# Fixed PSUM turns beside the FFN, and other places in SBUF for buffers of its last batch

## The chip, the cores and the metric

One core of a Trainium2 chip runs the whole program. The metric is the device time of one execution in microseconds (us), the median of three runs. The core has five engines that run side by side and wait for each other only through semaphores: PE (TensorE, matmuls into PSUM), DVE (VectorE), ACT (ScalarE), POOL (GpSimd) and SP (SyncE, which here only issues loads). PSUM has eight banks of 512 fp32 values in each of 128 partitions, and this kernel uses all of them.

## The reference

Two parts follow each other. The first is a long convolution over the sequence (S = 12544, D = 128 channels, B = 4 batches), done by FFT, with a filter that a small MLP makes; the second is a maxout FFN on every token (50176 tokens, d_ff = 768).

```python
h_filt = (np.maximum(pos_emb @ w1, 0.0) @ w2) * np.exp(-0.01 * pos)[:, None]
u = x * v
y = irfft(rfft(u, n=2*S, axis=1) * rfft(h_filt, n=2*S, axis=0)[None], n=2*S, axis=1)[:, :S]
a = (x * y).reshape(B * S, D)
h = np.maximum(np.maximum(a @ w1, a @ w2), a @ w3)    # the FFN's own w1, w2, w3
out = h @ w_out
```

All data is fp32. The kernel folds the three-way maximum: with w1 taken off w2 and w3, `h = max(0, a(w2-w1), a(w3-w1)) + a w1`, and the last term goes through one 128x128 matrix `lin = w1 w_out`. So each step of the FFN is two matmuls, pa and pb, a relu of pa, and a maximum of that with pb.

## The kernel before

**Stages.** The first 321 us make the filter's spectrum and convolve batch 0. Then the FFN runs batch by batch. While the FFN of batch b runs, the convolution of batch b+1 is done beside it, in between its steps; the FFN of the last batch has nothing beside it and is computed in a Strassen-like form (seven products for eight), in pairs of tiles.

**Tiles and steps.** A batch has 32 tiles of 392 tokens. A tile starts with `t_load` (zt, the convolution's last but one stage from DRAM, and xT, the gate x), `t_sums` (a sum and a difference of zt's halves: `even` and zt), and `t_last`: 64 small matmuls with the table `f4p` into a PSUM tile `yps`, and DVE's product with xT into the SBUF tile `gt`, the FFN's input. Then come six steps f = 0..5 of `up` and `down`. `up` runs pa, the relu on ACT into `hid` (L701), pb, and the maximum on DVE (L704); `down`, two steps later, adds `hid` times a slice of `w_out` to the bank `ops`. After the last step ACT copies `ops` to the SBUF tile `ot` and POOL stores it. A matmul of `up` is done as two column halves that run at the same time (`halves_mm`, L154).

**The convolution beside it.** `conv_steps` lays out 192 slots, one per FFN step, and gives every piece of the next batch's convolution a slot, by hand-set loads. The pieces that use PSUM are `u_first` (tile ps1, the first transform), and `g_quarter` (tile psq: matmuls L462 of the forward and L472 of the inverse quarter transform), which `g_fold` reads with ACT (eo) and DVE (cb). `q_unfold` (L518, DVE) makes the input xs of L472.

**What sets the order.** The program text does: instructions are issued on each engine in the order in which Python makes them, and the framework adds the waits. A tile is taken from a pool with a tag and a number of buffers; which of the free buffers it gets is the framework's choice at the time of the build, by its own estimate of what is free, and a tile waits for all users of the buffer's tile before it. When a pool is closed, its memory is given to pools opened later, and their first writers wait for its last users.

**PSUM while the FFN runs.** Three banks belong to pool `hps` (tag `hps`: pa and pb), two double banks to `cps` (tag `cv`: ps1, psq and yps), one bank to `ops`. For the last batch the double banks are closed and three single banks (`cps2`, for yps) and two for the products are opened.

**SBUF.** After the first stage closes its pools (`pro.close()`, which frees `eye`, the weights `w_sb0`, the spectrum `specH` and more), the pool `hp` is opened and holds f4p, sign, zt, xT, even, gt and hid; f4p and sign are loaded on ACT's queue, in `hp`'s first bytes. The pools of the convolution follow, with `op` (ot) among them. When they close after the third batch, pool `lp` opens in their place with all that the last batch needs: the sums of weights `tw` and `linx` (five subtractions on DVE, L1090, ahead of the last batch's first step), its relu buffers (tags h11, h21, h22, h12), and its output buffers.

Of the kernel before, what the change touches and what calls it, by code (L numbers as in the profile page):

```python
# [1 line left out]

# [7 lines left out]
FP32 = mybir.dt.float32  # L10
I32 = mybir.dt.int32
U16 = mybir.dt.uint16
ALU = mybir.AluOpType
ACTF = mybir.ActivationFunctionType
PSUM = bass.MemoryType.PSUM
P = 128
# [8 lines left out]
N1 = 90  # L25
# [64 lines left out]
def kernel(  # L90
# [15 lines left out]
    nc = tc.nc  # L106
    NG, _, _, B, NB = x.shape
# [21 lines left out]
    f4p_d = nc.inline_tensor(np.ascontiguousarray(f4p_t), name="f4p_const").ap()  # L129
    wt_d = nc.inline_tensor(w_t, name="wt_const").ap()  # L130
    wq_d = nc.inline_tensor(wq_t, name="wq_const").ap()
    sign = np.where(np.arange(N1) < NK, 1, -1).astype(np.float32)[:, None]
    sign_d = nc.inline_tensor(sign.copy(), name="sign_const").ap()
# [6 lines left out]
    lin = const.tile([D, D], FP32, name="lin")  # L140
# [258 lines left out]
    def u_first(u, i0=0, n=4):  # L399


        t = uts[u] if i0 + n < 4 else uts.pop(u)
        ps = cps.tile([P, 256 * n], FP32, tag="cv", name="ps1")
        at = 4 * u + i0
        for i in range(n):
            for h in range(2):
                for c in range(2):
                    nc.tensor.matmul(  # L408
                        ps[64 * c:64 * c + 64, 256 * i + h * N1:256 * i + (h + 1) * N1],
                        t[:, 2 * ((at + i) % 8) + h].rearrange("n r t -> n (r t)"),  # L410
                        f1q[:, h, c * N1:(c + 1) * N1],
                        start=(i % 2 == 0 and h == 0), stop=True, skip_group_check=True)
        v = ps[:].rearrange("p (s m) -> p s m", m=256)[:, :, 0:2 * N1].rearrange(
            "p s (h k) -> p h k s", h=2)
        high = cvp.tile([P, n, D], FP32, tag="eo", name="high", bufs=2)
        high = high[:, :, 0:N1].rearrange("p s k -> p k s")
        nc.scalar.copy(high, v[:, 0])  # L417
        for a, op in enumerate((ALU.add, ALU.subtract)):
            nc.vector.tensor_tensor(out=spec[:, :, a, at:at + n], in0=v[:, 1], in1=high, op=op)  # L419
# [32 lines left out]
    def g_quarter(g, z):  # L452


        ps = cps.tile([P, 1024], FP32, tag="cv", name="psq")
        if g is not None:
            w, t = ws.pop((g, 0)), sqs.pop(g)
            for k in range(2):
                for r in range(2):
                    for a in range(2):  # L460
                        at = 512 * r + k * D
                        nc.tensor.matmul(  # L462
                            ps[64 * a:64 * a + 64, at:at + D], w[64 * r:64 * r + 64, k, a, :],
                            t[64 * r:64 * r + 64, k, a, :], start=(k == 0), stop=True,
                            skip_group_check=True)
        if z is not None:
            w, ab = ws.pop((z, 1)), abs_.pop(z)
            for q in range(2):
                for a in range(2):
                    for k in range(2):  # L470
                        at = 512 * a + 256 + q * D
                        nc.tensor.matmul(  # L472
                            ps[64 * k:64 * k + 64, at:at + D], w[64 * a:64 * a + 64, k, q, :],
                            ab[64 * a:64 * a + 64, q, k, :], start=(g is None and q == 0),
                            stop=True, skip_group_check=True)
        pss[g, z] = ps
# [160 lines left out]
    N = 4 * NB  # L637
# [38 lines left out]

    def t_last(i):
        zt = zts.pop(i)
        ps = cps.tile([P, state["yps"]], FP32, tag="cv", name="yps")
        own = i[0] == B - 1 and i[1] > 1  # L680
        g = (lp if own else hp).tile([D, 4, NB], FP32, tag="g", name="gt", bufs=4 if own else 3)
        y = ps[:, 0:N].rearrange("d (p n) -> d p n", p=4)

        h = NB // 2
        for s in range(4):
            for a in range(2):
                halves_mm(y[:, s, a * h:a * h + h], zt[a][:, s * D:(s + 1) * D],
                          f4p[:, i[0] > 0 and i[1] >= NT // 2, a, :], s == 0 and a == 0, True)
        y = y.rearrange("d p (a m) -> d p m a", a=2)
        xT = xTs.pop(i)  # L690
        nc.vector.tensor_tensor(out=g[:].rearrange("d p (m a) -> d p m a", a=2), in0=y,  # L691
                                in1=xT.rearrange("d p (m a) -> d p m a", a=2),
                                op=ALU.mult)
        gs[i] = g

    def up(i, f, tag="hid", bufs=3):
        rhs = gs[i][:].rearrange("d p n -> d (p n)")
        h = (lp if tag[0] == "h" and tag != "hid" else hp).tile([P, N], FP32, tag=tag, name="hid", bufs=bufs)
        pa = hps.tile([P, 512], FP32, tag="hps", name="pa")
        halves_mm(pa[:, 0:N], w_sb[1][:, f * P:(f + 1) * P], rhs, True, True)  # L700
        nc.scalar.activation(h[:], pa[:, 0:N], Relu)  # L701
        pb = hps.tile([P, 512], FP32, tag="hps", name="pb")
        halves_mm(pb[:, 0:N], w_sb[2][:, f * P:(f + 1) * P], rhs, True, True)
        nc.vector.tensor_tensor(out=h[:], in0=h[:], in1=pb[:, 0:N], op=ALU.max)  # L704
        return h
# [20 lines left out]
    NC = NF // 2  # L726
    ORDER = (("h11", 0), ("h21", 0), ("h11", 1), ("h22", 0), ("h21", 1), ("h11", 2),
             ("h21", 2), ("h22", 1), ("h22", 2), ("h12", 0), ("h12", 1), ("h12", 2))
    BUFS = {"h11": 3, "h21": 4, "h22": 4, "h12": 3}
# [167 lines left out]
    for i in (1, 2):  # L897
        nc.vector.tensor_tensor(out=w_sb[i][:], in0=w_sb[i][:], in1=w_sb[0][:],
                                op=ALU.subtract)
# [3 lines left out]
    cvp = pro.enter_context(tc.tile_pool(name="cvp0", bufs=3))  # L903
    cps = pro.enter_context(tc.tile_pool(name="cps0", bufs=3, space=PSUM))
    gps = pro.enter_context(tc.tile_pool(name="gps", bufs=2, space=PSUM))
    sps = pro.enter_context(tc.tile_pool(name="sps", bufs=1, space=PSUM))
    state = {"cv": (cvp, cps), "turn": cps, "xb": 2}
    pl = sps.tile([D, 512], FP32, name="pl")
    Gs, minus = {}, {}

# [103 lines left out]
    pro.close()  # L1014


    hp = ctx.enter_context(tc.tile_pool(name="hp", bufs=3))
    conv = ExitStack()
    f4p = hp.tile([N1, 2, 2, NB // 2], FP32, name="f4p", bufs=1)
    nc.scalar.dma_start(f4p[:], f4p_d)  # L1020
    sign_t = hp.tile([N1, 1], FP32, name="sign", bufs=1)
    nc.scalar.dma_start(sign_t[:], sign_d)
    inq = conv.enter_context(tc.tile_pool(name="inq", bufs=1))
    op_ = conv.enter_context(tc.tile_pool(name="op", bufs=2))
    wp = conv.enter_context(tc.tile_pool(name="wp", bufs=3))
    hh = conv.enter_context(tc.tile_pool(name="hh", bufs=2))
    cvp = conv.enter_context(tc.tile_pool(name="cvp", bufs=3))
    hps = ctx.enter_context(tc.tile_pool(name="hps", bufs=3, space=PSUM))
    cps = conv.enter_context(tc.tile_pool(name="cps", bufs=2, space=PSUM))
    ops = conv.enter_context(tc.tile_pool(name="ops", bufs=1, space=PSUM))  # L1030
    state = {"yps": 1024}


    tiles = [(b, i) for b in range(B) for i in range(NT)]
# [40 lines left out]


    lp = ctx.enter_context(tc.tile_pool(name="lp", bufs=1))
    cps = ctx.enter_context(tc.tile_pool(name="cps2", bufs=3, space=PSUM))
    state["yps"] = 512
    ops = ctx.enter_context(tc.tile_pool(name="ops2", bufs=1, space=PSUM))  # L1080
    banks = [ops.tile([P, 512], FP32, name=f"ops{i}") for i in range(2)]

# [2 lines left out]
    linx = lp.tile([D, 64], FP32, name="linx", bufs=1)  # L1085
    b11, b12 = wo_sb[:, 0:NC, 0:64], wo_sb[:, 0:NC, 64:128]
    b21, b22 = wo_sb[:, NC:, 0:64], wo_sb[:, NC:, 64:128]
    for out, a, b in ((tw[:, 1], b22, b12), (b12, b12, b11), (tw[:, 0], b22, b12),
                      (tw[:, 2], b21, tw[:, 0]), (linx[:], lin[:, 0:64], lin[:, 64:128])):
        nc.vector.tensor_tensor(out=out, in0=a, in1=b, op=ALU.subtract)  # L1090

    stream = {}

# [4 lines left out]
    for i in range(0, NT, 2):  # L1098
        h = {}
        X, Y = banks if i % 4 == 0 else banks[::-1]  # L1100
        for j, (name, f) in enumerate(ORDER):
            n = int(name[1]) - 1
            if j < 2 and i + 2 < NT:
                t_load(b, i + 2 + j)
            h[name, f] = first if step == 0 else up(
                (b, i + n), f + (NC if name[2] == "2" else 0), name, BUFS[name])
            if j == 0:
                entries = products(b, i, h, X, Y)
                for q, e_ in enumerate(entries):
                    at_ = step + LAG + q * NSTEP // len(entries)  # L1110
                    for fn in e_:
                        if isinstance(fn, tuple):
                            later(at_ + 1, *fn)
                        elif fn is not None:
                            later(at_, fn)
                for at_, (fn, c) in SUMS.items():
                    later(step + at_, fn, h, c)
            run(stream.pop(step, ()))
            if j in (3, 6) and i + 2 < NT:
                t_sums((b, i + 2 + (j > 3)), nc.vector)  # L1120
            if j in (5, 8) and i + 2 < NT:
                t_last((b, i + 2 + (j > 5)))
            step += 1
# [39 lines left out]
```

## Time and profile before

Times: 2338.91 us, the median of 2336.47, 2338.91 and 2343.64. The profiled execution took 2339.31 us, with a span of 2337.5 us and a mean granted PE clock of 0.996.

| stretch of the span, us | length | PE busy | DVE busy | ACT busy | POOL busy | DMA share |
|---|---|---|---|---|---|---|
| 340 to 820 (FFN beside the convolution) | 480.00 | 471.06 | 336.04 | 268.09 | 211.09 | 0.90 |
| 820 to 830 (end of batch 0) | 10.00 | 6.95 | 5.25 | 1.52 | 3.16 | 0.11 |
| 830 to 1911.65 (FFN beside the convolution) | 1081.65 | 1073.13 | 775.97 | 582.27 | 376.16 | 0.90 |
| 1911.65 to 1925 (start of the last batch) | 13.35 | 9.86 | 6.18 | 2.87 | 3.75 | 0.13 |
| 1925 to 2330 (last batch) | 405.00 | 404.78 | 193.54 | 102.96 | 263.29 | 0.22 |

The table sums each engine's busy time in a stretch. A busy PE in it is one whose matmuls follow each other; their ends are modelled, so two that overlap count once, and a gap between starts tells more than the busy share. Lines of the timeline begin with start and duration in us, then the engine, the line of the kernel, the operation, what is written and read, the shape, and how many are merged; in square brackets stands how long the engine was idle before it and what ended that. "SPq" and "ACTq" are the queues that issue loads. Names lose their numbers, so ps1 is shown as ps.

### The profile page before, as it was taken

The numbers are of one execution on the slowest core, as the hardware profiler recorded it, in microseconds if no ns is written. First come the engines' busy times: TensorE is split into PE (matmuls) and PEld (weight loads), VectorE is DVE, ScalarE is ACT, GpSimd is POOL, SyncE is SP. The second block draws the span as 40 slices with busy tenths as digits, with TensorE's granted clock in tenths as the row PEclk, the third lists the DMA queues.
The fourth block names the chain that finished last, engine by engine and source line by source line (L and its number), as shares of the span: only waits on it lengthen the run. The fifth ranks groups of instructions, "written<-read, shape, count | busy, mean of one in ns | idle before, by whom it ended". The sixth has DMA issues, their size and how long they took to land.

```text
span 2337.5 us, 68165 instructions
## 1 busy us (share of the span) xinstructions
PE 2284.1 (98%) x27853; PEld 1371.9 (59%) x27853; DVE 1553.8 (66%) x2798; ACT 1178.8 (50%) x2124; POOL 969.0 (41%) x1153
## 2 busy tenths in 40 slices
PE   8999989999999999999999999999999999999998
PEld 7889856655455445655555546655555546666665
DVE  5678856656777746757888846757888855454443
ACT  2678844456666624446666634446666622222222
POOL 1045424424444424324333324324333326666666
PEclk9999999999999999999999999999999999999999
DMA  7868969989998749979999849969999822222221
GB/s 160 201 202 266 290 158 181 165 180 238 226 238 219 198 104 187 188 141 238 240 248 246 226 113 180 192 144 244 242 241 245 223 80 66 54 54 70 65 55 22
DMA packets 473146, 410.93 MB, mean 176 GB/s; under 512 B 328004, under 2 KB 374231, under 8 KB 472834
## 3 DMA queue, kind: packets, MB, share of 16 engines
q1 hardware_dynamic: 433504, 317.61, 62.2%
q0 software_dynamic: 26400, 75.72, 11.2%
q10 hardware_dynamic: 12930, 13.25, 1.8%
q8 instruction: 219, 3.59, 0.7%
q14 instruction: 93, 0.76, 0.1%
HBM read 262.77 MB, written 84.67 MB: 149 GB/s over the span
## 4 chain that ended last, share of the span: by engine, by line
PE 76%; DMA 11%; DVE 5%; issue 3%; ACT 2%; SPq 1%; POOL 0%; ACTq 0%; DVEq 0%; POOLq 0%
PE pa L154 18%; PE pb L154 17%; PE ops L154 14%; PE ops L764 6%; PE ps L408 5%; DMA ht<-hd 4%; PE yps L154 4%; PE ps L163 3%; PE ps L154 2%; DMA zt<-zd 2%; PE psq L472 2%; DVE xs L518 2%; PE psq L462 2%; DMA sq<-spec 2%; DMA wt<-wq_const 1%
## 5 line engine op out<-in xcount | busy, mean ns | idle before, releaser
L701 ACT ACTIVATE hid<-pa 128x392 f32<-128x392 f32 x768 | 383.5, 499 | 756.5 <-PE pa L154 738.3
L704 DVE TENSOR_TENSOR hid<-hid,pb 128x392 f32<-128x392 f32 x768 | 428.2, 558 | 361.9 <-PE pb L154 351.5
L154 PE MATMUL pb<-gt,w_sb 128*64 128x392 f32 x3072 | 640.3, 495 | 10.2 <-ACT hid L701 10.2
L154 PE MATMUL pa<-gt,w_sb 128*64 128x392 f32 x3072 | 644.8, 497 | 0.7 <-DVE gt L691 0.7
L154 PE MATMUL ops<-hid,wo_sb 128*64 128x392 f32 x2304 | 478.1, 493 | 0.0
L154 PEld LDWEIGHTS pb<-gt,w_sb 128*64 128x64 f32 x3072 | 220.6, 137 | 301.2 <-issue 263.2
L514 POOL TENSOR_TENSOR cb<-cb,xs 128x512 f32<-128x512 f32 x135 | 176.3, 1306 | 455.1 <-DVE xs L511 210.5
L154 PEld LDWEIGHTS ops<-hid,wo_sb 128*64 128x64 f32 x2304 | 167.0, 137 | 212.9 <-issue 212.9
L154 PEld LDWEIGHTS pa<-gt,w_sb 128*64 128x64 f32 x3072 | 200.6, 137 | 147.6 <-issue 124.4
L419 DVE TENSOR_TENSOR spec<-ps,high 128x360 f32<-128x360 f32 (+1 forms) x204 | 142.1, 739 | 131.2 <-ACT high L417 130.8
L487 DVE TENSOR_TENSOR cb<-psq,eo 128x512 f32<-128x512 f32 (+1 forms) x288 | 175.3, 650 | 75.1 <-ACT eo L484 74.6
L719 POOL DMA_DIRECT2D out_dram<-ot x96 | 75.3, 785 | 322.2 <-ACT ot L717 293.7
L502 ACT ACTIVATE xs<-cb 32x512 f32<-32x512 f32 x270 | 169.9, 629 | 22.2 <-DVE cb L487 13.4
L518 DVE TENSOR_TENSOR xs<-cb 128x256 f32<-128x256 f32 x270 | 167.5, 662 | 9.8 <-POOL cb L514 9.8
L503 ACT COPY xs<-cb 32x512 f32<-32x512 f32 x270 | 166.7, 617 | 3.2
L417 ACT COPY high<-ps 128x360 f32<-128x360 f32 (+1 forms) x102 | 77.2, 761 | 157.2 <-PE ps L408 126.3
L408 PEld LDWEIGHTS ps<-f1q,uT 98*64 98x64 f32 x3072 | 131.8, 137 | 35.2 <-issue 32.9
L154 PEld LDWEIGHTS yps<-f4p,even 90*64 90x64 f32 x2048 | 116.1, 139 | 40.9 <-issue 35.0
L408 PE MATMUL ps<-f1q,uT 98*64 98x90 f32 x3072 | 136.4, 241 | 3.2 <-DVE spec L419 2.6
L691 DVE TENSOR_TENSOR gt<-yps,xT 128x392 f32<-128x392 f32 x128 | 72.3, 565 | 91.7 <-PE yps L154 52.6
L154 PE MATMUL yps<-f4p,even 90*64 90x49 f32 x2048 | 125.7, 221 | 3.0 <-DMA f4p<-f4p_const 3.0
L154 PE MATMUL yps<-f4p,zt 90*64 90x49 f32 x2048 | 127.3, 223 | 0.0
(130 smaller groups left out, 3306.7 us busy)
## 6 DMA issues: line engine op xcount, KB each, us to landing
ht<-hd SPq DMA_DIRECT2D x264, 256.0 KB, 6.7
wt<-wq_const SPq DMA_DIRECT2D x144, 256.0 KB, 6.4
zd<-cb POOLq DMA_DIRECT2D x135, 256.0 KB, 6.2
zt<-zd SPq DMA_DIRECT2D x384, 90.0 KB, 3.1
sq<-spec SPq DMA_DIRECT2D x264, 128.0 KB, 7.0
ut<-in_xr_dram SPq DMA_DIRECT2D x128, 196.0 KB, 4.3
ut<-in_vr_dram SPq DMA_DIRECT2D x128, 196.0 KB, 4.6
xT<-in_x_dram SPq DMA_DIRECT2D x256, 98.0 KB, 3.6
```

The lines of the kernel that those rows point to most:

```text
L154: nc.tensor.matmul(out[64 * h:64 * h + 64], lhsT[:, 64 * h:64 * h + 64], rhs, start=start, stop=stop, skip_group_check=True)
L408: nc.tensor.matmul(ps[64 * c:64 * c + 64, 256 * i + h * N1:256 * i + (h + 1) * N1], t[:, 2 * ((at + i) % 8) + h].rearrange("n r t -> n (r ...
L417: nc.scalar.copy(high, v[:, 0])
L419: nc.vector.tensor_tensor(out=spec[:, :, a, at:at + n], in0=v[:, 1], in1=high, op=op)
L487: nc.vector.tensor_tensor(out=cb[:, a, lo:hi], in0=ps[:, lo:hi], in1=eo[:, lo:hi], op=op)
L502: nc.scalar.mul(xs[at:at + 32], xt[at + 32:at + 64], -1.0)
L503: nc.scalar.copy(xs[at + 32:at + 64], xt[at:at + 32])
L514: nc.gpsimd.tensor_tensor(out=xts[g], in0=xts[g], in1=xs[:], op=ALU.add)
L518: nc.vector.tensor_tensor(out=ab[:, q], in0=y[:, 0], in1=y[:, 1], op=(ALU.subtract, ALU.add)[q])
L701: nc.scalar.activation(h[:], pa[:, 0:N], Relu)
L704: nc.vector.tensor_tensor(out=h[:], in0=h[:], in1=pb[:, 0:N], op=ALU.max)
L764: nc.tensor.matmul(ps[64 * c:64 * c + 64, 0:H2], w, rhs[:, H2 * c:H2 * c + H2], start=start, stop=True, skip_group_check=True)
```

## The change

Four things change; what is computed, and the instructions that compute it, stay the same.

1. The PSUM tiles of the FFN and of what runs beside it become fixed tiles that are used in strict turns: `hbanks` cycles over three single banks for pa, pb, pa, pb and so on; `pairs` cycles over two double banks for ps1, psq and yps; `singles` over three single banks for yps in the last batch. A matmul into such a tile waits for the readers of that tile alone. The first stage keeps its pool behind the same call (`state["bank"]`).
2. `hid` moves to a pool of its own, `hidp`, opened ahead of `hp`. f4p and sign thereby lie 4704 bytes higher, where specH was, and are loaded on SP's queue ahead of the first zt instead of on ACT's.
3. The pool `op` of ot is opened outside the convolution's pools, so its memory is not given to `lp`. The first three relu buffers of the last batch (steps 0 to 2) come from `hidp` instead of `lp`.
4. The five subtractions that make `tw` and `linx` are no longer made ahead of the last batch's first steps but one each behind `up` in steps 3 to 7.

The purpose is that no tile waits for a buffer that only the choice of the pool gave it, and that the last batch can start while the last store of the batch before is still under way.

```diff
         t = uts[u] if i0 + n < 4 else uts.pop(u)
-        ps = cps.tile([P, 256 * n], FP32, tag="cv", name="ps1")
+        ps = state["bank"]()[:, 0:256 * n]
         at = 4 * u + i0
...
                         start=(i % 2 == 0 and h == 0), stop=True, skip_group_check=True)
-        v = ps[:].rearrange("p (s m) -> p s m", m=256)[:, :, 0:2 * N1].rearrange(
+        v = ps.rearrange("p (s m) -> p s m", m=256)[:, :, 0:2 * N1].rearrange(
             "p s (h k) -> p h k s", h=2)
...
     def g_quarter(g, z):
-        ps = cps.tile([P, 1024], FP32, tag="cv", name="psq")
+        ps = state["bank"]()
         if g is not None:
...
         zt = zts.pop(i)
-        ps = cps.tile([P, state["yps"]], FP32, tag="cv", name="yps")
+        ps = state["bank"]()
         own = i[0] == B - 1 and i[1] > 1
...
         rhs = gs[i][:].rearrange("d p n -> d (p n)")
-        h = (lp if tag[0] == "h" and tag != "hid" else hp).tile([P, N], FP32, tag=tag, name="hid", bufs=bufs)
-        pa = hps.tile([P, 512], FP32, tag="hps", name="pa")
+        h = (hidp if tag == "hid" else lp).tile([P, N], FP32, tag=tag, name="hid", bufs=bufs)
+        pa = next(hbanks)
         halves_mm(pa[:, 0:N], w_sb[1][:, f * P:(f + 1) * P], rhs, True, True)
         nc.scalar.activation(h[:], pa[:, 0:N], Relu)
-        pb = hps.tile([P, 512], FP32, tag="hps", name="pb")
+        pb = next(hbanks)
         halves_mm(pb[:, 0:N], w_sb[2][:, f * P:(f + 1) * P], rhs, True, True)
...
     sps = pro.enter_context(tc.tile_pool(name="sps", bufs=1, space=PSUM))
-    state = {"cv": (cvp, cps), "turn": cps, "xb": 2}
+    state = {"cv": (cvp, cps), "turn": cps, "xb": 2,
+             "bank": lambda: cps.tile([P, 512], FP32, tag="cv", name="ps1")}
     pl = sps.tile([D, 512], FP32, name="pl")
...
     pro.close()
+    hidp = ctx.enter_context(tc.tile_pool(name="hidp", bufs=3))
     hp = ctx.enter_context(tc.tile_pool(name="hp", bufs=3))
+    f4p = hp.tile([N1, 2, 2, NB // 2], FP32, name="f4p", bufs=1)
+    nc.sync.dma_start(f4p[:], f4p_d)
+    sign_t = hp.tile([N1, 1], FP32, name="sign", bufs=1)
+    nc.sync.dma_start(sign_t[:], sign_d)
+    op_ = ctx.enter_context(tc.tile_pool(name="op", bufs=2))
     conv = ExitStack()
-    f4p = hp.tile([N1, 2, 2, NB // 2], FP32, name="f4p", bufs=1)
-    nc.scalar.dma_start(f4p[:], f4p_d)
-    sign_t = hp.tile([N1, 1], FP32, name="sign", bufs=1)
-    nc.scalar.dma_start(sign_t[:], sign_d)
     inq = conv.enter_context(tc.tile_pool(name="inq", bufs=1))
-    op_ = conv.enter_context(tc.tile_pool(name="op", bufs=2))
     wp = conv.enter_context(tc.tile_pool(name="wp", bufs=3))
     cvp = conv.enter_context(tc.tile_pool(name="cvp", bufs=3))
-    hps = ctx.enter_context(tc.tile_pool(name="hps", bufs=3, space=PSUM))
-    cps = conv.enter_context(tc.tile_pool(name="cps", bufs=2, space=PSUM))
+    hps = ctx.enter_context(tc.tile_pool(name="hps", bufs=1, space=PSUM))
+    cps = conv.enter_context(tc.tile_pool(name="cps", bufs=1, space=PSUM))
     ops = conv.enter_context(tc.tile_pool(name="ops", bufs=1, space=PSUM))
-    state = {"yps": 1024}
+    hbanks = itertools.cycle([hps.tile([P, 512], FP32, name=f"hps{i}") for i in range(3)])
+    pairs = itertools.cycle([cps.tile([P, 1024], FP32, name=f"cps{i}") for i in range(2)])
+    state = {"bank": lambda: next(pairs)}
     tiles = [(b, i) for b in range(B) for i in range(NT)]
...
     lp = ctx.enter_context(tc.tile_pool(name="lp", bufs=1))
-    cps = ctx.enter_context(tc.tile_pool(name="cps2", bufs=3, space=PSUM))
-    state["yps"] = 512
+    cps = ctx.enter_context(tc.tile_pool(name="cps2", bufs=1, space=PSUM))
+    singles = itertools.cycle([cps.tile([P, 512], FP32, name=f"last{i}") for i in range(3)])
+    state = {"bank": lambda: next(singles)}
     ops = ctx.enter_context(tc.tile_pool(name="ops2", bufs=1, space=PSUM))
...
     b21, b22 = wo_sb[:, NC:, 0:64], wo_sb[:, NC:, 64:128]
-    for out, a, b in ((tw[:, 1], b22, b12), (b12, b12, b11), (tw[:, 0], b22, b12),
-                      (tw[:, 2], b21, tw[:, 0]), (linx[:], lin[:, 0:64], lin[:, 64:128])):
-        nc.vector.tensor_tensor(out=out, in0=a, in1=b, op=ALU.subtract)
+    weights = [(tw[:, 1], b22, b12), (b12, b12, b11), (tw[:, 0], b22, b12),
+               (tw[:, 2], b21, tw[:, 0]), (linx[:], lin[:, 0:64], lin[:, 64:128])]
     stream = {}
...
                 t_load(b, i + 2 + j)
+            own = (name, BUFS[name]) if step > 2 else ("hid", 3)
             h[name, f] = first if step == 0 else up(
-                (b, i + n), f + (NC if name[2] == "2" else 0), name, BUFS[name])
+                (b, i + n), f + (NC if name[2] == "2" else 0), *own)
+            if step > 2 and weights:
+                out, a1, a2 = weights.pop(0)
+                nc.vector.tensor_tensor(out=out, in0=a1, in1=a2, op=ALU.subtract)
             if j == 0:
```

More of the change, by code (lines that the diff above doesn't have):

```diff
@@ L1 @@
+import itertools
 from contextlib import ExitStack
```

## The prediction

> **What bounds the kernel now.** I read the page first: PE is busy 2284.1 of 2337.5 us (98%), DVE 66%, ACT 50%. In the two FFN parts matmul blocks start every 0.66 us, each block being two column halves of 392 columns that run side by side, and between 1925 and 2330 us PE is busy 404.78 of 405.00 us. So time can only come from the few gaps on PE. The view of waits on PE names them (us in total, times, longest):
> ```profile
> PE pb L154 <- ACT hid L701: 10.2, 12, 3.5
> PE psq L472 <- DVE xs L518: 9.6, 15, 1.0
> ...
> PE yps L154 <- DMA f4p<-f4p_const: 3.0, 1, 3.0
> PE psq L472 <- DVE gt L691: 3.0, 1, 3.0
> ```
> Row 1 is a matmul that waits for a relu to empty its PSUM bank (one entry is 3.5, the rest about 0.6 each), row 2 a quarter transform that waits for its data. The timeline then shows each kind. First a short one:
> ```profile
> 614.56 0.83 PE L154 MATMUL pb<-gt,w_sb 128*64 128x392 f32 x4
> 615.87 0.83 PE L154 MATMUL pa<-gt,w_sb 128*64 128x392 f32 x4
> 617.30 0.88 PE L154 MATMUL pb<-gt,w_sb 128*64 128x392 f32 x4 [0.60 <-ACT hid L701]
> ```
> The second pb starts 1.43 us after its own pa instead of 0.66: both were put in the same bank, so it waits until the relu (L701) has read pa. Next the change to the last batch, all engines:
> ```profile
> 1912.70 0.76 POOL L719 DMA_DIRECT2D out_dram<-ot  x1 [11.30 <-ACT ot L717]
> 1912.96 0.83 PE L154 MATMUL pa<-gt,w_sb 128*64 128x392 f32 x4
> 1916.60 0.36 DVE L1090 TENSOR_TENSOR tw<-wo_sb 128x192 f32<-128x192 f32 x1 [5.42 <-DMA out_dram<-ot]
> 1916.70 0.89 ACT L701 ACTIVATE hid<-pa 128x392 f32<-128x392 f32 x2 [4.31 <-DMA out_dram<-ot]
> 1917.25 1.57 PE L154 MATMUL pb<-gt,w_sb 128*64 128x392 f32 x4 [3.46 <-ACT hid L701]
> ...
> 1918.62 1.52 PE L154 MATMUL pa<-gt,w_sb 128*64 128x392 f32 x4
> ...
> 1923.56 0.27 PE L154 MATMUL yps<-f4p,even 90*64 90x49 f32 x4
> ```
> The weight sums and the relu write SBUF that the closed convolution pools gave back, that of the output buffer ot among it; they wait until its last store has landed, and PE waits for the relu. After the gap the blocks start 1.37 and 1.30 us apart. The start of the first FFN:
> ```profile
> 320.51 1.92 SPq L645 DMA_DIRECT2D zt<-zd  x2
> ...
> 324.22 0.63 ACTq L1020 DMA_DIRECT2D f4p<-f4p_const  x1
> ...
> 325.53 0.69 DVE L669 TENSOR_TENSOR even<-zt 90x512 f32<-90x512 f32 x1 [0.30 <-DMA zt<-zd]
> 326.26 0.69 DVE L670 TENSOR_TENSOR zt<-zt 90x512 f32<-90x512 f32 x1
> 327.11 0.46 PE L154 MATMUL yps<-f4p,even 90*64 90x49 f32 x4 [3.05 <-DMA f4p<-f4p_const]
> ```
> The table f4p lands last, but `even` was ready only 0.9 us earlier (326.22).
>
> **What the skill says.** "PSUM — Partial Sum Buffer", PSUM bank collisions: access by two engines must be guarded by bank and quadrant, not by address. That is why a pb in its pa's bank has to wait for the whole relu; the trace agrees (pb starts 0.05 us after the relu's end). The same page, Engine vs sequencer instructions: the VectorE and ScalarE queues are strict FIFO; the trace agrees: the max at 1918.19 stands behind five weight sums. "TensorE: Matmul & The Clock Gate", Part 1: after an idle window of about 3.4 us the array runs at half clock until it has been busy about as long; the trace agrees (1.30 against 0.66 us). "Perfetto Trace Analysis", Identifying the Most-Contended Engine: repeated equal bubbles can mean too few buffers. Here the number is enough, the choice of buffer makes the bubble.
>
> **The change, part by part.** The order of instructions is the same on PE, ACT and POOL but for the two table loads, which go from ACT's queue to SP's; on DVE the five sums move. What changes is waits and addresses. I compared both built programs' waits, instruction by instruction, and placed each new wait on the times of this trace.
>
> 1. *Three FFN banks in turns.* The order is pa, pb, pa, pb, so pb of step k takes the bank of pa of step k-1 (waits for that relu) and pa of step k the bank of pb of step k-2 (waits for that max). In the kernel before, 10 of the 768 pairs share one bank: pa at 343.7, 346.5, 615.9, 746.6, 870.5, 873.3, 1395.9, 1398.7 (pb 1.43 later) and 571.9, 702.6 (1.73 later). Against 0.66 that is 8 x 0.77 + 2 x 1.07 = 8.3 us. The blocks after them start 0.71 instead of 0.66 later: 10 x 0.05 = 0.5. In turns pb needs the relu before, which in these ten places ended 0.8 us or more ahead of it. **Gain 8.8.**
> The turns also bind. At 1118, 1199, 1295, 1643, 1725 and 1821 us the max that pa must now await ends 0.67 us after pa's start. One of them:
> ```profile
> 1198.84 0.83 PE L154 MATMUL pa<-gt,w_sb 128*64 128x392 f32 x4
> 1198.97 0.55 DVE L704 TENSOR_TENSOR hid<-hid,pb 128x392 f32<-128x392 f32 x1
> 1199.58 0.88 PE L154 MATMUL pb<-gt,w_sb 128*64 128x392 f32 x4
> ...
> 1203.00 0.45 PE L472 MATMUL psq<-xs,wt 64*64 64x128 f32 x8 [0.41 <-DVE xs L518]
> ```
> That is 6 x 0.67 = 4.0 lost. But DVE runs without a pause there from 1196.3, and 3 us later psq waits for DVE anyway (starting 0.65 late at four of the six, 0.45 at two: 3.5 in all); a later PE meets the same DVE. Net 0.5, less the 0.06 waits of pb that go: **0.3 lost**, bounds 0 and 4.0. All other new waits on PE have 0.7 us or more to spare (but for pa at 1918.62, whose max comes earlier with part 3), those on ACT 1.3 or more, so they cost nothing.
> 2. *Two double banks in turns* (psq, yps, ps1): with two buffers in alternation the same reader is awaited; no wait of PE on another engine is new. **0**; the 3.0 us at 820 stays, since psq there needs the bank of yps either way.
> 3. *First relu buffers, ot and the sums of the last batch.* Relu 578 and 579 now wait for maxima that ended 2.6 us or more before them, and the sums stand one per step behind the max, waiting for nothing. From pa at 1912.96 to yps at 1923.56 it took 10.60 us; eight blocks at 0.66 take 5.3. Gain 5.3, of which DVE may take back up to 0.6: a step is 1.31 us and carries 0.56 + 0.36 on DVE, plus the two sums of zt (0.68 and 0.69 to 1.39) before yps. **Gain 5.1.** The sums are needed from step 9 on and are done in step 7.
> 4. *f4p and sign on SP's queue, ahead of zt.* f4p waits for the same fold matmul that zt waited for (320.4), so it starts at 320.51 and takes 0.63, sign 0.34. Every load behind them (zt, xT) moves 0.97. f4p then lands at 320.51 + 2.8 = 323.3, off the path, but zt lands at 326.5, `even` ends at 327.2, the difference at 327.9 and yps ends at 329.7 instead of 329.1. **0.6 lost**, bounds 0 and 1.0. On ACT nothing stood behind the two loads (next relu at 331.5), so leaving it gains nothing.
>
> Sum: 8.8 - 0.3 + 5.1 - 0.6 = 13.0; 2338.9 - 13.0 = **2326**.
>
> **Rivals.**
> - *The turns' gain is absorbed* (chance 0.19): PE runs earlier into waits on DVE xs (9.6 us in 15 places). With all of it absorbed, 2338.9 - 5.1 + 0.6 = 2334; with half, 2330. For it: DVE is at 70% there. Against it: after the psq blocks at 503.25, 633.94 and 764.62 the next block comes 1.35 us late each time, though 18 us ahead of the first there is no bank stall, and ahead of the others there is one. So that wait moves with PE.
> - *The gap at 820 goes too* (0.10): psq waits for gt, gt for three DVE sums (L518) that took 4.64 us beside POOL's t_sums, against 0.66 each on the page. A shift of a microsecond may part them: 3.3 + 1.8 of slow clock gives 2321.
> - *More such gaps* (0.05): the shift brings that meeting to all three batch ends, or the first FFN's gap grows: 2326 + 3 x 5.1 = 2341, slower.
>
> **How the numbers follow.** My forecast has 0.66. Its own bounds are 2325 (nothing lost in 1 and 4) and 2330 (4.0 lost in 1); the runs of before scatter by some 3 us either way (2336.5 to 2343.6). The range reaches from the 820 case to full absorption, 2320 to 2334; only the slower case and part of the scatter are left out. Faster by 0.3% means below 2331.9: the forecast, half of the absorption case and the 820 case, 0.66 + 0.09 + 0.10, about 0.84. The other half of the absorption makes most of the 0.12 within 0.3%; the last case leaves 0.04 for slower.
>
> **What would show it.** Turns: the row "pb <- ACT hid" of PE's waits falls from 10.2 to under 1, and no pb starts 1.4 us after its pa. Binding: a row "pa <- DVE hid" of about 4 us in six waits, with the psq row shorter by about as much. Last batch: no wait on out_dram on ACT or DVE after 1900 us, yps about 5.3 us after the same pa. Start: yps waits for the sums of zt and not for f4p, and starts no earlier. I am wrong if psq's waits grow by what the banks save, if DVE's moved sums delay the first yps of the last batch by over 1 us, or if new PE gaps over 3 us appear.

## The result, and the profile after

The kernel after takes 2327.08 us (median of 4 runs, 2326.81 to 2328.18), beside 2339.88 us for the kernel before (median of 4, 2336.47 to 2343.64): ratio 0.9946, 95% interval 0.9929 to 0.9963, or 12.8 us. Repeated in later rounds beside 25 runs of the kernel before: 2329.16 against 2341.04 us, ratio 0.9954 (0.9942 to 0.9967). The profiled spans are 2325.0 and 2337.5 us, 12.5 apart.

The view of waits on PE, kernel after (us in total, times, longest), to be held against the four rows shown of before; psq and yps are now called cps, pa and pb are hps, and all lines moved by one:
```profile
PE cps L473 <- DVE xs L519: 7.5, 9, 1.0
PE hps L155 <- DVE hid L705: 3.3, 6, 0.6
PE cps L473 <- DVE gt L692: 3.0, 1, 3.0
PE cps L155 <- DVE even L670: 2.9, 1, 2.9
...
PE last L155 <- DVE zt L671: 0.7, 2, 0.4
```
No row hps <- ACT hid is left. In its place stand six waits of hps for the max. The gap for gt is as long as it was. The last row is new: two yps of the last batch wait for the sums of zt.

The change to the last batch, from the timeline of all engines:
```profile
1904.75 0.76 POOL L720 DMA_DIRECT2D out_dram<-ot  x1 [11.31 <-DMA zt<-zd]
...
1910.33 0.32 PE L155 MATMUL last<-f4p,even 90*64 90x49 f32 x4
1910.97 0.32 PE L155 MATMUL last<-f4p,zt 90*64 90x49 f32 x4 [0.31 <-DVE zt L671]
...
1915.74 0.69 DVE L671 TENSOR_TENSOR zt<-zt 90x512 f32<-90x512 f32 x1
1916.48 0.32 PE L155 MATMUL last<-f4p,zt 90*64 90x49 f32 x4 [0.40 <-DVE zt L671]
```
The store of ot is still under way, and nobody waits for it. The yps of before's 1923.56 starts at 1910.33.

The start of the first FFN:
```profile
320.63 0.38 SPq L1022 DMA_DIRECT2D f4p<-f4p_const  x1
321.07 0.35 SPq L1024 DMA_DIRECT2D sign<-sign_const  x1
321.60 1.99 SPq L646 DMA_DIRECT2D zt<-zd  x2
...
327.11 0.32 PE L155 MATMUL cps<-f4p,even 90*64 90x49 f32 x4 [2.95 <-DVE even L670]
327.83 0.46 PE L155 MATMUL cps<-f4p,zt 90*64 90x49 f32 x4 [0.40 <-DVE zt L671]
```
zt is issued 1.0 us behind f4p. The first yps starts when it did, but now waits for `even`, and its second pair of operands comes 0.72 us after the first. The first pa starts at 330.32 in place of 329.81.

The two traces hold the same matmuls in the same order, so the start of the same yps in both tells what has been gained up to there (minus: lost):

| landmark | before | after | gained |
|---|---|---|---|
| first pa | 329.81 | 330.32 | -0.51 |
| last yps ahead of the last batch's first FFN block | 1908.08 | 1900.13 | +7.95 |
| next yps, behind the gap of before | 1923.56 | 1910.33 | +13.23 |
| the one after it | 1928.67 | 1915.78 | +12.89 |
| the third | 1947.99 | 1935.50 | +12.49 |
| end | 2337.50 | 2325.01 | +12.49 |

So the FFN beside the convolution gained 7.95 + 0.51 = 8.46 us, the last batch 5.28 and then lost 0.74 of it again, and the start lost 0.51. After 1935 us the two traces run alike. These are one execution of each kernel; the next section shows by how much others differ.

### The profile page after: what moved, and what is told of

Its sections match the earlier page's. It is cut to its first block, busy times and chain, and to the rows that moved or that the text cites. A ratio compares the mean times of both kernels' runs of the same rounds, so it can differ in the third digit from the quotient of the medians.

```text
span 2325.0 us, 68379 instructions
## 1 busy us (share of the span) xinstructions
PE 2282.1 (98%) x27853; PEld 1378.6 (59%) x27853; DVE 1551.9 (67%) x2798; ACT 1178.9 (51%) x2124; POOL 967.3 (42%) x1153
## 4 chain that ended last, share of the span: by engine, by line
PE 82%; DMA 5%; DVE 5%; issue 3%; ACT 3%; SPq 1%; ACTq 0%; POOL 0%; DVEq 0%; POOLq 0%
PE hps L155 40%; PE ops L155 16%; PE ops L765 6%; PE cps L409 5%; PE cps L155 4%; PE ps L164 3%; PE cps L473 2%; PE cps L463 2%; DVE xs L519 2%; PE last L155 1%; DMA ht<-hd 1%; DMA hd<-ht 1%; ACT ht L958 1%; PE pm L324 1%; PE pst L362 1%
## 5 line engine op out<-in xcount | busy, mean ns | idle before, releaser
L155 PE MATMUL hps<-gt,w_sb 128*64 128x392 f32 x6144 | 1151.0, 495 | 4.1 <-DVE hid L705 3.3
L702 ACT ACTIVATE hid<-hps 128x392 f32<-128x392 f32 x768 | 384.2, 500 | 747.8 <-PE hps L155 732.2
L155 PEld LDWEIGHTS hps<-gt,w_sb 128*64 128x64 f32 x6144 | 423.5, 137 | 436.5 <-issue 397.7
L705 DVE TENSOR_TENSOR hid<-hid,hps 128x392 f32<-128x392 f32 x768 | 427.6, 557 | 356.5 <-PE hps L155 346.5
L515 POOL TENSOR_TENSOR cb<-cb,xs 128x512 f32<-128x512 f32 x135 | 176.2, 1305 | 452.9 <-DVE xs L512 207.1
L488 DVE TENSOR_TENSOR cb<-cps,eo 128x512 f32<-128x512 f32 (+1 forms) x288 | 175.1, 649 | 74.8 <-ACT eo L485 74.3
L420 DVE TENSOR_TENSOR spec<-cps,high 128x360 f32<-128x360 f32 x180 | 135.1, 792 | 121.7 <-ACT high L418 121.7
L519 DVE TENSOR_TENSOR xs<-cb 128x256 f32<-128x256 f32 x270 | 167.2, 661 | 9.8 <-POOL cb L515 9.8
L409 PEld LDWEIGHTS cps<-f1q,uT 98*64 98x64 f32 x2880 | 124.2, 137 | 31.3 <-issue 29.8
L409 PE MATMUL cps<-f1q,uT 98*64 98x90 f32 x2880 | 127.7, 241 | 0.4 <-DVE uT L393 0.4
L155 PE MATMUL cps<-f4p,even 90*64 90x49 f32 x1568 | 96.3, 221 | 2.9 <-DVE even L670 2.9
L507 DVE TENSOR_TENSOR cb<-cb,ht 128x512 f32<-128x512 f32 x135 | 93.3, 691 | 8.1 <-ACT xs L504 7.6
```

The costliest lines, as they stand in the source:

```text
L155: nc.tensor.matmul(out[64 * h:64 * h + 64], lhsT[:, 64 * h:64 * h + 64], rhs, start=start, stop=stop, skip_group_check=True)
L409: nc.tensor.matmul(ps[64 * c:64 * c + 64, 256 * i + h * N1:256 * i + (h + 1) * N1], t[:, 2 * ((at + i) % 8) + h].rearrange("n r t -> n (r ...
L488: nc.vector.tensor_tensor(out=cb[:, a, lo:hi], in0=ps[:, lo:hi], in1=eo[:, lo:hi], op=op)
L507: nc.vector.tensor_tensor(out=xts[g], in0=xts[g], in1=hts[g][:, 0].rearrange("p k q d -> p q k d"), op=ALU.mult)
L515: nc.gpsimd.tensor_tensor(out=xts[g], in0=xts[g], in1=xs[:], op=ALU.add)
L519: nc.vector.tensor_tensor(out=ab[:, q], in0=y[:, 0], in1=y[:, 1], op=(ALU.subtract, ALU.add)[q])
```

## The experiments

Each ratio is to the kernel before on the same chip in the same rounds. Its runs scatter from 2335.5 to 2346.4 us over the three groups, with medians of 2340.7 to 2341.0, so differences of a microsecond or two are read from the landmarks of the trace, not from the times.

### The banks alone

```diff
-        pa = hps.tile([P, 512], FP32, tag="hps", name="pa")
+        pa = next(hbanks)
...
-        pb = hps.tile([P, 512], FP32, tag="hps", name="pb")
+        pb = next(hbanks)
```


> The kernel before with one part of the change: pa and pb take the three hps banks in strict turns; the op pool, the table, the first relus and the sums stay where they were. My theory (each part acts alone, and the turns are worth 8.5 us, measured as 7.95 us at the first pa of the last batch plus the 0.51 us that the change lost at the start): 8.5 us faster than the kernel before, 2331 us. The row "pb <- ACT hid" falls from 12 waits and 10.2 us to the one of about 3.5 us in the last batch, and a row hps <- DVE hid of six waits and about 3.3 us appears. Rival (the ten stalls merely moved slack, and part of the 8.5 us came from the other parts): under 6 us faster.

Measured: 2333.58 us, ratio 0.9971 (0.9961 to 0.9981), 6.8 us by the ratio. In the trace the first pa is 1.14 us later than in the kernel before (the stage ahead of it ended later in this execution) and the yps of 1908.08 is 5.78 us earlier: 6.9 us gained. From 340 to 881 us it follows the kernel after to 0.1 us; then it loses 0.28 us at 1342, and 0.96 near 1572, where psq waits for its loads (sq 0.7, wt 0.6). The row pb <- ACT hid shrank to the one wait of 3.3 us in the last batch, as expected, and hps <- DVE hid has 3.9 us in seven. The turns act alone. Their size in this run is 1.6 us under the 8.5 of the theory, of which the trace puts 1.2 down to those two stretches, the loads among them.

How far one pair of executions can be read shows in the same stretch, from the first pa to the yps of 1908.08, in the other profiles. With the turns it is shorter than in the profile of the kernel before by 8.46 us in the first profile of the kernel after, 7.10 in its second, 6.9 here, and 6.26 and 6.38 in two kernels below that do the same there (the table on GpSimd's queue, the sums earlier). Without the turns it is 1.73 and 0.51 longer (the output buffer, the relus and sums) and 0.18 shorter (the pairs). With the kernel before among the latter, the means are 7.5 us apart.

### The pairs of banks alone

```diff
-        ps = cps.tile([P, 1024], FP32, tag="cv", name="psq")
+        ps = state["bank"]()
```
(and the same for ps1 and yps)

> The kernel before with one part of the change: the pairs of banks of psq, ps1 and yps, and the three single banks of the last batch, in strict turns; the hps pool and everything else as before. Theory of the prediction (each of these banks was free in time, and the 3.0 us wait for gt is no wait for a bank): no difference to the kernel before beyond what two executions differ, under 2 us, and the same rows in the waits. Rival (the turns change which bank the convolution's products take, and cost or save stalls): rows of psq or yps with another releaser, 3 us or more either way.

Measured: 2340.70 us, ratio 0.9998 (0.9988 to 1.0008). The waits name the same releasers, psq <- DVE xs 9.3 us in 15 and the gap for gt of 3.0. This part does nothing, as step 2 had it.

### The output buffer alone

```diff
+    op_ = ctx.enter_context(tc.tile_pool(name="op", bufs=2))
     hp = ctx.enter_context(tc.tile_pool(name="hp", bufs=3))
...
-    op_ = conv.enter_context(tc.tile_pool(name="op", bufs=2))
```


> The kernel before with one part of the change: the op pool, which holds ot, is opened outside the pools that close before the last batch, so that no tile of the last batch lies where the store of ot reads. The first relus, the sums and the hps banks stay as they were. Theory (the wait on the store of ot is the sole cause of the 3.5 us gap of the last batch): the 3.5 us wait and the half clock after it go, 4.5 to 5.3 us faster than the kernel before, about 2335 us, and no wait on out_dram after 1900 us. Rival (the relus' and the sums' places in SBUF wait for something else that ends nearly as late): under 2 us faster, with a wait of another name in the same place.

Measured: 2334.55 us, ratio 0.9976 (0.9967 to 0.9986), 5.6 us. In the trace this kernel is 1.85 us behind the kernel before at the yps of 1908.08 and 3.48 us ahead of it at that of 1923.56, and stays at 3.49: 5.33 us gained there and nothing given back. Between 1900 and 1940 us PE waits for nobody, and no engine for out_dram. The store of ot alone made the gap.

### The relus and the sums alone

```diff
-        h = (lp if tag[0] == "h" and tag != "hid" else hp).tile([P, N], FP32, tag=tag, name="hid", bufs=bufs)
+        h = (hidp if tag == "hid" else lp).tile([P, N], FP32, tag=tag, name="hid", bufs=bufs)
...
+            own = (name, BUFS[name]) if step > 2 else ("hid", 3)
...
+            if step > 2 and weights:
+                out, a1, a2 = weights.pop(0)
+                nc.vector.tensor_tensor(out=out, in0=a1, in1=a2, op=ALU.subtract)
```


> The kernel before with the two other moves of the last batch: the first relus in the pool hidp outside and the sums one by one behind steps 3 to 7; the op pool stays inside, the hps banks as before. Theory (the store of ot is what the wait is for, and the first relu that lies on freed SBUF waits for it): the relu of step 3 takes over the wait, until the store has landed at about 1916 us, so that the stop comes some two pairs later and is shorter, 1 to 1.5 us in place of 3.5: 2 to 4 us faster than the kernel before, with a row hps <- ACT hid after 1912 us. Rival (moving the relus is what matters, and the store is never waited for again): about 5 us faster and no such row. With the op pool apart alone the gain in this stretch was 5.34 us, so the relus and the sums cannot add more than what is lost to the sums, 0.4 us.

Measured: 2337.08 us, ratio 0.9983 (0.9977 to 0.9990), 4.0 us. In the trace 4.16 us are gained from the yps of 1908.08 to that of 1923.56 and 0.82 given back by the yps of 1947.99: 3.34 net. The timeline shows the store still holding a relu, now that of a later step:
```profile
1918.32 0.89 ACT L701 ACTIVATE hid<-pa 128x392 f32<-128x392 f32 x2 [2.21 <-PE pa L154]
1918.33 1.02 POOL L734 TENSOR_TENSOR s<-hid 128x392 f32<-128x392 f32 x1 [3.09 <-DMA out_dram<-ot]
...
1918.87 0.88 PE L154 MATMUL pb<-gt,w_sb 128*64 128x392 f32 x4 [0.67 <-ACT hid L701]
```
The relu and GpSimd's first op start within 10 ns of each other, GpSimd behind the store; the profile puts the relu's wait down to its pa, which began at 1916.06 and lasted 0.83. PE meanwhile had other blocks to do and waited 0.67 us, less than the 1 to 1.5 expected. So this half of part 3 moves the wait behind work, and moving ot removes it. With ot outside, the relus add nothing, and the late sums cost the 0.74 us that the kernel after gives back: the output buffer alone keeps its 5.33, the full part 3 ends at 4.54 (and at 5.33 again with the sums made earlier, below).

### A bank for pa alone

```diff
-        pa = next(hbanks)
+        pa = abank
...
-    hbanks = itertools.cycle([hps.tile([P, 512], FP32, name=f"hps{i}") for i in range(3)])
+    abank, *bbanks = [hps.tile([P, 512], FP32, name=f"hps{i}") for i in range(3)]
+    hbanks = itertools.cycle(bbanks)
```


> The kernel after with the turns changed in one way: pa has one of the three banks for itself and pb alternates between the two others, so pb's bank is free two pairs later. Theory of the prediction (a binding turn shifts 0.67 us of waiting from psq to pa, and the wait for psq absorbs it again): within 0.6 us of the kernel after, since the waits at the six places (1111, 1192, 1288, 1635, 1716, 1812 us) only move back to psq <- xs. Rival (what the six turns cost, 4 us, was really lost): 3 to 4 us faster than the kernel after. A third outcome, worse by several us, would mean that pa now waits for the relu of the pair before it.

Measured: 2336.44 us, ratio 0.9981 (0.9975 to 0.9988): slower than the kernel after (0.9946, 0.9954) by some 6 to 8 us, 11.4 us in the trace. It is the third outcome: pa now waits for the relu of the pair before it (a row of 5.4 us in 14 waits), and sixteen tiles take 0.46 or 0.65 us longer each, 8.9 in all. But at the six binding places, where no such wait stands, it settles the dispute. Here is one, pa own bank first, then the kernel after, PE's timeline:
```profile
1198.29 1.49 PE L155 MATMUL hps<-gt,w_sb 128*64 128x392 f32 x8
...
1200.27 1.61 PE L155 MATMUL hps<-gt,w_sb 128*64 128x392 f32 x8
...
1204.41 0.45 PE L473 MATMUL cps<-xs,wt 64*64 64x128 f32 x8 [0.41 <-DVE xs L519]
...
1205.67 1.54 PE L155 MATMUL hps<-gt,w_sb 128*64 128x392 f32 x8
```
```profile
1190.62 1.49 PE L155 MATMUL hps<-gt,w_sb 128*64 128x392 f32 x8
...
1193.33 1.54 PE L155 MATMUL hps<-gt,w_sb 128*64 128x392 f32 x8 [0.56 <-DVE hid L705]
...
1198.02 1.54 PE L155 MATMUL hps<-gt,w_sb 128*64 128x392 f32 x8
```
(A row of x8 is a pa with its pb.) Freed from the max, pa starts 1.98 us after the pa before it instead of 2.71, and then psq waits 0.41 for xs. At the pa behind psq both stand at the same place: 7.38 and 7.40 us from the first line. Between the yps around the six places the kernel after takes 0.19, 0.02, 0.01, 0.20, 0.02 and 0.02 us longer, 0.46 in all, and 0.4 longer than the kernel before. The waits were absorbed.

### The table on GpSimd's queue

```diff
-    nc.sync.dma_start(f4p[:], f4p_d)
+    nc.gpsimd.dma_start(f4p[:], f4p_d)
...
-    nc.sync.dma_start(sign_t[:], sign_d)
+    nc.gpsimd.dma_start(sign_t[:], sign_d)
```


> The kernel after with f4p and sign loaded on GpSimd's queue and not ahead of zt on the sync queue. Theory (the two loads' issue on SP, 0.97 us of time, made zt land later, and yps waits for the sums of zt): zt lands about 1 us earlier, even starts at about 325.4 and the first yps at about 326.2 us in place of 327.11, everything behind it moves by the same, 2326 us, 0.5 to 1.0 us faster than the kernel after. Rival (the first yps is then held by f4p itself, which landed at 327.1 in the kernel before): no gain, and the wait of the first yps is put down to f4p.

Measured: 2328.85 us, ratio 0.9951 (0.9939 to 0.9964): no difference to the kernel after that the times can tell. The first pa is 0.80 us earlier than in the kernel after, but 0.58 of it was there already at SP's first issue (320.05, against 320.63), which this edit doesn't touch. So the fair measure is the first pa from SP's first issue behind the prologue, in all profiles:

| loads of f4p and sign | first pa after SP's first issue, us | mean |
|---|---|---|
| on ACT's queue (before, banks, pairs, output buffer, relus) | 9.30, 9.28, 9.43, 9.59, 9.29 | 9.38 |
| on SP's queue (after twice, pa own bank, two runs below) | 9.69, 9.84, 9.82, 9.76, 9.65 | 9.75 |
| on GpSimd's queue (this one, two runs below) | 9.47, 9.55, 8.92 | 9.31 |

The move of the loads to SP costs about 0.4 us and GpSimd's queue takes it back. `even` came at 325.56, not 325.4: it starts 5.51 us after the first issue of zt, against 4.76 in the kernel after (326.36 behind 321.60). Why was not tried.

### The sums of the last batch earlier

```diff
-            if step > 2 and weights:
+            for _ in range(min(2, len(weights)) if step < 3 else 0):
```


> The kernel after with the five sums of the last batch (tw, linx) placed two, two and one behind the steps 0 to 2 in place of one behind each of the steps 3 to 7. Theory (two of the sums stand on DVE ahead of the sums even and zt, and make the first two yps of the last batch late by 0.3 and 0.4 us): no row last <- DVE zt, 0.4 to 0.7 us faster than the kernel after, seen in the trace from the first pa of the last batch on. Rival: the earlier sums make the maxima of steps 0 to 2 late and pa waits there instead, no gain.

Measured: 2328.09 us, ratio 0.9951 (0.9938 to 0.9963), not apart from the kernel after in the times. In the trace the row last <- DVE zt is gone, and the yps of 1900.13 and 1935.50 are 34.58 us apart instead of 35.37: 0.79 us, a little more than expected. The five sums' late places were the cause of the 0.74.

### The gap at 816 us

In the kernel after, GpSimd does the sums of the tile behind n = 30 beside the first FFN step of that n. One edit puts them one step later:
```diff
-            if f == (3 if turn_ else 0):
+            if f == (3 if turn_ else 1 if n == 30 else 0):
```


> The kernel after with one edit: the sums even and zt of the one tile with n = 30, which GpSimd does at 815.25 to 818.0 us, go one step later. In the kernel after DVE's three xs sums (L519) beside them take 4.63 us together, and elsewhere four take 2.50. Theory (the two engines hinder each other there, so that DVE comes late to gt and max, and PE waits 3.0 us for gt at 819 us with half the clock afterwards): the three sums take about 1.9 us, the wait for gt goes or falls below 1 us, and the kernel is 3 to 4.5 us faster than the kernel after, 2323 to 2324 us. Rival (DVE is late there for another reason, a product or a load): the wait of 3.0 us stays and the time is the same.

Measured: 2322.57 us (2322.32 to 2324.43), ratio 0.9926 (0.9914 to 0.9939); the kernel after had 2329.16 in the same rounds. First the kernel after, then this one, DVE, GpSimd and PE:
```profile
813.66 4.63 DVE L519 TENSOR_TENSOR xs<-cb 128x256 f32<-128x256 f32 x3
...
815.25 1.36 POOL L670 TENSOR_TENSOR even<-zt 90x512 f32<-90x512 f32 x1
...
816.68 1.33 POOL L671 TENSOR_TENSOR zt<-zt 90x512 f32<-90x512 f32 x1
818.22 0.55 DVE L705 TENSOR_TENSOR hid<-hid,hps 128x392 f32<-128x392 f32 x1
818.70 0.55 DVE L692 TENSOR_TENSOR gt<-cps,xT 128x392 f32<-128x392 f32 x1
819.30 1.13 PE L473 MATMUL cps<-xs,wt 64*64 64x128 f32 x16 [3.04 <-DVE gt L692]
```
```profile
813.55 1.98 DVE L519 TENSOR_TENSOR xs<-cb 128x256 f32<-128x256 f32 x3
...
815.93 0.55 DVE L692 TENSOR_TENSOR gt<-cps,xT 128x392 f32<-128x392 f32 x1
816.53 0.67 PE L473 MATMUL cps<-xs,wt 64*64 64x128 f32 x16 [0.39 <-DVE gt L692]
```
The same three sums take 4.63 us beside GpSimd's two and 1.98 without them, and the wait falls from 3.04 to 0.39. PE's granted clock between 818 and 822 us goes from 0.63 to 1.00. The yps around it (799.51 and 833.94 in the kernel after) are 34.43 us apart in the kernel after and 30.29 here: 4.1 us. In three other profiles that have the gap (the kernel after again, the table on GpSimd's queue, the sums earlier) they are 35.5 to 35.8 apart, so it is worth up to 5.5. There the clock stays down longer behind a gap of the same 3.04 us: over the six us that follow it the granted clock is 0.74 in the first profile of the kernel after and 0.56 in the second. The 6.6 us of the times are more than the 3 to 4.5 expected: against the kernel after in the same rounds the trace puts 5.2 down to the gap, while 1.6 lie ahead of the first pa, which the edit does not touch.

The single sums show how. In the kernel after GpSimd ops end at 814.68 (L515), 816.61 and 818.02, and DVE's three sums end at 814.97, 816.90 and 818.30, each 0.28 to 0.29 us behind one of them. Over the whole kernel after 65 of the 270 xs sums take more than 0.5 us, 67 us in all over the 0.41 of a free one, and every one of the 65 ends 0.28 to 0.29 us behind a GpSimd sum. "SBUF — State Buffer" of the Trainium skill, SBUF: two separate sides, says that a VectorE op with two SBUF inputs and a GpSimd op that reads SBUF share one port pair as a lock: whichever starts first has it for its whole instruction, and the other blocks. The trace agrees that one of the two waits for the other: L519 has two inputs in SBUF; with one input in PSUM, L705 at 820.76 and L488 at 821.24 keep their 0.56 and 0.42 us beside GpSimd's op of 820.91 in the second kernel. It does not show that the first to start wins. By the recorded starts VectorE was first in 7 of the 65 (the sum held longest here begins at 814.89, GpSimd's at 815.25), and at 1194.72 us GpSimd's L515, first by 0.15 us, takes 1.70 in place of 1.27 us while VectorE's sum keeps its 0.42. So an op that has begun can be held by another engine's, beside the waits through semaphores, which the section on the cores names as the only ones.

### Three edits together, and GpSimd's sum on DVE

The three edits above in one kernel:

> The kernel after with three edits together: the sums of the tile n = 30 one step later, f4p and sign on GpSimd's queue, the five sums of the last batch two, two and one behind the steps 0 to 2. The first alone gave 2322.57 us; the trace showed 0.80 us at the first pa for the second, and 0.78 us in the last batch for the third. Theory (they lie in three different stretches and add up): 2322.57 - 0.80 - 0.78 = 2321.0 us. Rival (the start and the last batch are paid back at the next wait for a load): 2322.6 us as with the first alone.

Measured: 2323.88 us (2321.82 to 2325.02), ratio 0.9926 (0.9914 to 0.9939): no further gain that the times can tell. The trace shows 0.79 us in the last batch again. The 0.80 in the sum was mis-sized, since 0.58 of it was no effect of the edit (above). The two theories are 1.6 us apart, and five runs that scatter by 3 don't part them.

Then, since the xs sums that PE waits for stand beside GpSimd's sum L515:
```diff
-        nc.gpsimd.tensor_tensor(out=xts[g], in0=xts[g], in1=xs[:], op=ALU.add)
+        nc.vector.tensor_tensor(out=xts[g], in0=xts[g], in1=xs[:], op=ALU.add)
```


> The three edits of the run before it, and the sum cb = cb + xs (L515, 1.27 us on GpSimd) on DVE in its place. Theory (DVE's xs sums, L519, are held while a GpSimd sum runs and end 0.3 us after it; 65 of 270 took over 0.5 us, and the waits of cps for xs, 8 us in ten places, come from L515): with the sum on DVE, at about 0.69 us as L507 and L512 have it, the xs sums are back at 0.41 us beside it and the waits for xs shrink to under 4 us: 2 to 5 us faster than the run before it. Rival (DVE gains 33 sums of 0.69 us in the places where it is already late, and max and gt come later than the hold had made them): same or slower by up to 5 us, with the waits moved to hps <- DVE hid and gt.

Measured: 2344.72 us, ratio 1.0015 (1.0007 to 1.0023): 21 us slower than the run before it, four times what the rival allowed. The sum is done 135 times, not 33 as the expectation had it, which is 93 us on DVE at the 0.69 it takes there. The holds of L519 did shrink, from 63 to 13. But GpSimd's sums of zt now come beside a product:
```profile
532.91 2.13 DVE L507 TENSOR_TENSOR cb<-cb,ht 128x512 f32<-128x512 f32 x1
533.09 1.39 POOL L670 TENSOR_TENSOR even<-zt 90x512 f32<-90x512 f32 x1
```
That product takes 0.68 us elsewhere. Of the products L507 and L512, 27 take over 0.9 us, against 1 in the run before it; gt comes late behind it, and psq waits for gt 9.4 us in six places and for xs 16.6 us in thirteen. How much of the loss is the added work and how much the held products is not told apart. (5.1 of the profile's 24 us are lost between 60 and 70 us, ahead of anything edited.)

## Why the prediction was right, step by step

- **Turns of the FFN banks: held.** All ten stalls are gone, and no hps waits for a relu. Predicted 8.8 - 0.3 = 8.5; the landmarks of the first pair give 8.46, but that they agree to 0.04 us is luck: the executions with the turns give 6.3 to 8.5, and on average they are 7.5 us faster there than those without. The same three banks do without the ten stalls, so their number was enough, as the prediction said; its remark on equal bubbles stands in "Perfetto Trace Analysis" under Optimization Strategy, not in the section it names. That a pb had to wait for the relu follows already from its writing over the values that the relu reads; no run here tells a guard by bank from a guard by address.
- **The six binding places: held, which was the least certain term.** The row hps <- DVE hid has 3.3 us in six waits, for "about 4". Of the 4.0 us only 0.4 to 0.5 is lost. The 0.3 of the prediction does not follow from its own figures: 4.0 less 3.5 less six times 0.06 would be 0.1. The own bank for pa shows the exchange at 7.38 against 7.40 us. The row of psq did not fall by as much (9.6 to 7.5 us), since that view counts less than the starts show.
- **Pairs of banks: held,** 0.9998 alone. The gap at 820 stayed, at 816.
- **Last batch: the gain held, the price of the sums was mis-sized.** yps starts 5.28 us earlier for 5.3. What DVE takes back was put at 0.2 net, with 0.6 as the bound; it is 0.74. A sum of the weights (0.35 us) stands behind the max and ahead of `even` at both of the first two yps, so it is paid twice: the first waits 0.31 us for zt, the second 0.40. And of the three moves one does the work. The output buffer alone gives 5.33; relus and sums moved as well give 4.54.
- **Table on SP: held.** 0.51 in this pair of profiles, 0.4 over the ten that load it on ACT's or SP's queue, for 0.6. yps waits for the sums of zt, as said, and starts no earlier.
- **Rivals.** Absorption on DVE xs did not come: what the turns save up to 881 us is still there at 1900. The case of the gap at 820 did not come by itself, but its reading (three sums beside GpSimd's) was right, and one edit brought it about; only the 0.66 per sum that it took from the page is a mean over free sums of 0.41 and held ones. No new gap appeared.

Sum: 8.46 + 5.28 - 0.74 - 0.51 = 12.49, for 13.0. The second profile of the kernel after comes to 10.1 against the same profile of the kernel before, so the mechanism is shown for every part, and the total within some 2 us.

## What to carry to other kernels

Waits that a change removes or adds can be added up only after asking, for each, which wait comes next on the same engine: ten stalls on a relu were worth nearly their full length, since nothing else held PE there, and six new waits on DVE cost nearly nothing, since PE met the same DVE 3 us later. When several buffers are moved to end one wait, find the one whose last reader ends last; here the output buffer was enough, and the work rescheduled around the others cost more than it brought. Ahead of moving work from GpSimd to VectorE or back, look at which ops overlap in the timeline, not only at how busy each engine is.

## What the runs showed of the hardware

- A VectorE sum with two inputs in SBUF that is held by a GpSimd sum ends 0.28 to 0.29 us after it (65 of 65 in the kernel after), and takes up to 2.0 us for its own 0.41. In four more meetings there the VectorE sum kept its 0.41 and GpSimd's took 1.4 to 1.7 us for 1.27. One such meeting with the order of work against it cost 4.1 to 5.5 us of a kernel at 98% PE, the slow clock after the gap among it.
- A gap of 3.04 us on PE was enough for the slow clock (granted 1.00 over 818 to 819 us in the kernel after, 0.74 over the six us from 819.3), where the prediction speaks of an idle window of about 3.4 us. How long it stays down differs between executions, which moves the time by about 1 us.
- A relu held by a store was put down by the profile to a matmul that had long ended; GpSimd's op released at the same instant showed the real cause.
- The stage ahead of the first FFN ends at another time in each execution: SP's first issue behind it lies between 319.94 and 322.21 us in twelve profiles, and at 326.64 in one. One profile of each kernel cannot resolve a microsecond without a landmark that leaves this out.
